# A second buffer for the transposed row maxima, and the loads for eight heads put in the queue over eight head steps

## The chip, the cores and the metric

One core of a Trainium2 chip runs the kernel. The metric is the device time of one execution in microseconds; the profile adds one execution with a record of every instruction.

## What is computed

Two independent branches on 2048 x 576 inputs, concatenated along the last axis.

```python
# A: 32 heads of width 18, sequence in N=4 segments of L=512
q,k,v = x@wq, x@wk, x@wv                     # split in heads and segments
for s in range(4):
    logits = qs @ ks.T * 18**-0.5 + mask     # mask: -1e9 where key > query ... within the segment
    a_dot  = softmax(logits) @ vs
    a_mem  = phi(qs) @ M / (phi(qs) @ z + 1e-6)
    o      = g*a_mem + (1-g)*a_dot           # g = sigmoid(beta), one per head
    M += phi(ks).T @ vs; z += sum(phi(ks))   # phi(t) = t+1 for t>0, exp(t) otherwise
out_a = o @ wo
# B: a filter in the frequency domain
out_b = irfft2(rfft2(x_B) * (w_r + 1j*w_i))
```

(The mask compares the indices inside a segment; the kernel keeps the entries it allows through a table of its own.)

## The kernel before

The program runs in stages. First the forward transform of branch B and the projections of branch A are interleaved; q, k, v go to scratch tensors in device memory (`qkD`, `reD`, `vD`, and `pqD` for phi(q)). Then the inverse transform of B is interleaved with a prologue of the attention. The last 360 us or so are the attention (`attention`, L938), and the change lies there.

The attention is a software pipeline of **head steps** `t` = 0 to 132, one head of one segment each. Four steps make a quad `k`, eight steps a **group** `n`, that is eight heads of one segment; there are 16 groups, and four of them make a segment `g`. In step `t` the program emits, in an order written out by hand:

- `s1` (L646) for the head eleven steps ahead: matmuls of Q and K, and on VectorE the maxima of each row of logits (L661, L667), into tiles `mx`, `mg`;
- `s2` (L694) for head `t`: matmuls L702, L706, L707, L711 of K and Q, which here have two more rows (108 and 109) that hold the row maxima and so subtract them, and on ScalarE the exponentials L703, L708, L712 into `P`; GpSimd zeroes the forbidden triangle (L716);
- `pv` (L731) for a quad some steps back, `pv_out` (L737) copies the result to `U`.

The row maxima get into rows 108 and 109 of Q by `mpath` (L675), once for each quad `k`, started two quads ahead. At the first step of the quad in progress VectorE and ScalarE finish the maxima and GpSimd splits them in two bf16 parts `mh` (L682, L683). At the second step TensorE transposes `mh` (L686) and ScalarE copies the result to `mts` (L689), of which there is one buffer. Two steps after that call's clock, which is the end of the third step of the quad, ScalarE issues the transfer from `mts` into Q (L692). `later(k, f)` puts a call off by k steps; `due(t)`, at the end of step `t`, makes the calls that have come due. In the prologue GpSimd issues that transfer (L691).

Loads for the steps to come stand in a list `q`. When a group begins (`t%8==0`) nine entries are appended (L960 to L963): four that load Q for the group two ahead (three pieces from `qkD`, L635, and the rest from `reD`, L637), four of the same kind that load K for the group three ahead, and the load of V for the group two ahead (`load_v`, L644). Each step takes one entry at its beginning (L982) and one at its end (L1005), so that the nine are in after four and a half steps. Q has three buffers, K four, V three. The Q just loaded is read first by `s1` at the sixth step of the same group (`t+11`); its buffer was last read by `s2` in the last step of the group before.

A second list, `qu`, is treated in the same way and holds the five stores of a finished group's `U` (L742 to `rD`, L747 to `uD`). They are appended at the end of the fourth step. All of these go to SyncE's (SP's) queue, and so do the loads of phi(q) (`pq`, L776), of unnormalized outputs (`ux`, L825), the chains of reciprocals (`recip`, L749: load L752, store L765, load L769), the stores of denominators (L790), some moves between tiles (L843, L844) and the stores of the output (`ya`, L877). SP works through its queue in program order and stands where a transfer has to wait for data or for a free buffer. Within the same part of the program only the `mts` transfer is in ScalarE's queue. In the program as built, every transfer of SP and ScalarE counts on one of eight semaphores that are dealt out in turn, in the order in which the framework's planner expects the issues; before an issue the queue waits until the transfer that had the same semaphore eight turns earlier has landed.

The tiles named `x` in the trace are those of Q, K and the mask that share one allocation (`x0`); `Qs<-mts` and `x<-mts` are the same line for different Q buffers.

Of the kernel before, what the change touches and what calls it, by code (L numbers as in the profile page):

```python
# [340 lines left out]
BF=mybir.dt.bfloat16  # L341
# [43 lines left out]
class ATT:  # L385
# [289 lines left out]
    def mpath(s,k):  # L675

        nc=s.nc; n,qd=divmod(k,2); Q=s.Qs[n%3]
        mx=s.mx.pop(k); mg=s.mg.pop(k)
        nc.vector.tensor_reduce(out=mg[:,:,2:3],in_=mx[:,:,:3],axis=mybir.AxisListType.X,op=OP.max)
        nc.scalar.copy(mg[:,:,0:1],mx[:,:,3:])  # L680
        mh=s.mh; mg=mg.rearrange("p h i -> p (h i)")
        nc.gpsimd.tensor_copy(mh[:,0],mg)  # L682
        nc.gpsimd.tensor_tensor(mh[:,1],mg,mh[:,0],op=OP.subtract)  # L683
        yield
        pt=s.psm.tile([128,1024],BF,name="mt",tag=s.mtag)[:,:128]
        nc.tensor.transpose(pt,mh.rearrange("p a m -> p (a m)"),s.idb)  # L686
        yield
        mt=s.sm.tile([32,128],BF,name="mts",bufs=1)
        nc.scalar.copy(mt,pt[:32])  # L689
        out=Q[108:110,4*qd:4*qd+4].rearrange("p h (i c) -> p (h i) c",c=128)  # L690
        if s.now<0: nc.gpsimd.dma_start(out,mt)  # L691
        else: s.later(2,lambda: nc.scalar.dma_start(out,mt))  # L692
        yield
# [244 lines left out]
    def attention(s,tp,ps):  # L938
        nc=s.nc; s.tp,s.ps,s.psm,s.mtag=tp,ps,s.ps1,"s1"
        s.homes()  # L940
        def steps(gen,i):
            for _ in range(i):
                try: next(gen)
                except StopIteration: return
        m=None
        q=[]
# [3 lines left out]
        def run_bg(rate):  # L950
            state["acc"]+=rate
            if state["acc"]>=1:
                state["acc"]-=1
                while bg:
                    try: next(bg[0]); break
                    except StopIteration: bg.pop(0)
        lane=[]
        for t in range(133):
            k,hh=divmod(t,4); n,qd=divmod(k,2); g=k//8
            if hh==0 and qd==0:  # L960
                if 0<n<14: q+=s.stack_dmas(n+2,0)
                if 0<n<13: q+=s.stack_dmas(n+3,1)
                if n+2<16: q.append(lambda n=n: s.load_v(n+2))  # L963
            st=t%32
            if 16<=t<21: s.pq_load(1,ORD[t-16])
            if t==34: bg.append(s.den(1,lane))
            if st==8 and g>0:
                def ln(g=g):
                    r=s.recip(s.rD[g-1],s.rrD[g-1],s.g1,False,"rr",2)
                    for i in range(8):  # L970
                        if 2<i<6: s.ux_load(g-1,ORD[i-3])
                        next(r); yield
                    yield from r
                    bg.append(s.mixed(g))
                    o=s.oproj(g-1)
                    if g<3: bg.append(itertools.islice(o,4)); bg.append(s.den(g+1,lane))
                    bg.append(o)
                lane.append(ln())
            if t==125: lane.append(s.recip(s.rD[3],s.rrD[3],s.g1,False,"rr"))
            a=s.s1(t+11) if t+11<128 else iter(())  # L980
            b=s.s2(t) if t<128 else iter(())
            if q: q.pop(0)()  # L982
            if qu: qu.pop(0)()
            steps(a,1)
            steps(b,1)
            run_bg(0)
            steps(a,1)
            steps(b,1)
            if 4<=t-1<132: s.pv((t-5)//4,(t-5)%4)
            run_bg(1.2)  # L990
            steps(a,1)
            if hh==1 and m is not None: steps(m,1)
            steps(b,1)
            if hh==1 and m is not None: steps(m,1)
            if hh==0 and k+2<32: m=s.mpath(k+2); next(m)
            if t>=7 and t%4==3:
                s.pv_out((t-7)//4)
                if t%8==3:
                    u=s.u_dmas((t-11)//8)
                    if t<124: s.later(1,lambda u=u: qu.extend(u))  # L1000
                    else: qu+=u
            for l in list(lane):
                try: next(l)
                except StopIteration: lane.remove(l)
            if q: q.pop(0)()  # L1005
            if qu: qu.pop(0)()
            s.due(t)
        assert not q
# [144 lines left out]
```

## Time and profile before

| | |
|---|---|
| median of 3 runs | 717.85 us (716.23 to 718.08) |
| profiled execution | 717.86 us, span 716.2 us, granted clock 0.997 |
| TensorE busy | 681.5 us, 95% of the span |
| VectorE busy | 551.0 us, 77% |
| ScalarE busy | 450.6 us, 63% |
| GpSimd busy | 210.0 us, 29% |
| SP's transfers (queue q1) | 106.89 MB, 59.1% of 16 DMA engines |

The profile tells for each instruction when it ran, how long its engine had been idle before it, and what released it ("1.15 <-ACT P L703": 1.15 us idle, ended by ScalarE's line 703). "PEld" is the load of weights into TensorE. "SPq" and "ACTq" are transfers issued by SP and ScalarE; the time in such a row is the issue, not the transfer. In the chain of work a row "DMA a<-b" has the time from issue to landing. A row of a stretch gives, after its length, the busy time and number of instructions of PE, PEld, DVE, ACT and POOL, the granted clock, the DMA share and GB/s.

### The profile page before, as it was taken

To read this page: it belongs to the slowest core of one execution; us is meant where nothing else is said; L and a number is where in the kernel's file an instruction comes from. 1 tells how busy PE (TensorE), PEld (TensorE's weight loads), DVE (VectorE), ACT (ScalarE), POOL (GpSimd) and SP (SyncE) were. 2 spreads that over 40 slices of the span, in tenths; PEclk is the share of its full clock that TensorE was granted. 3 is DMA by queue.
4 is the path that set the end of the run, shared out by engine and by line. 5 is a ranking of instruction groups with operands and counts; after the bars stand their busy time and mean duration, and the time that the engine had idled before them with its cause. 6 is when DMAs were issued, how large, how long until landed. Compare 5 with 4: busy or idle time off the path is not lost.

```text
span 716.2 us, 14406 instructions
## 1 busy us (share of the span) xinstructions
PE 681.5 (95%) x4991; PEld 501.8 (70%) x4991; DVE 551.0 (77%) x1262; ACT 450.6 (63%) x986; POOL 210.0 (29%) x403
## 2 busy tenths in 40 slices
PE   5999999999999999999999799899999999999997
PEld 4988769879779879999844354444666445663487
DVE  6999979899699789787687687887656876577533
ACT  3665796585586575443378587767666776567521
POOL 5532000100200111665145233434323652235300
PEclk9999999999999999999999999999999999999999
DMA  9995555675384778999249787997757968252152
GB/s 311 295 279 159 149 140 185 189 196 181 112 245 143 188 209 283 221 241 260 94 134 195 146 160 149 191 193 162 168 111 163 207 150 168 60 149 66 27 160 76
DMA packets 71146, 123.80 MB, mean 173 GB/s; under 512 B 12184, under 2 KB 39174, under 8 KB 67482
## 3 DMA queue, kind: packets, MB, share of 16 engines
q1 hardware_dynamic: 64422, 106.89, 59.1%
q0 software_dynamic: 5632, 15.76, 8.1%
q8 instruction: 39, 0.64, 0.4%
q10 hardware_dynamic: 1020, 0.25, 0.2%
q14 instruction: 33, 0.27, 0.2%
HBM read 82.10 MB, written 39.81 MB: 170 GB/s over the span
## 4 chain that ended last, share of the span: by engine, by line
PE 62%; DMA 12%; ACT 4%; DVE 3%; issue 3%; POOL 3%; SPq 1%; ACTq 0%; POOLq 0%; DVEq 0%
PE pj L461 12%; PE pjv L461 8%; PE s L653 8%; PE pv L731 7%; PE po L874 4%; PE i L306 3%; PE i L295 3%; PE s L702 3%; DMA x<-mts 2%; DMA yb<-yout 2%; PE s L706 2%; PE pn L804 2%; PE pm L529 2%; PE s L666 1%; PE s L711 1%
## 5 line engine op out<-in xcount | busy, mean ns | idle before, releaser
L661 DVE CUSTOM_DVE_ANT_0 junk<-s,x 128x512 bf16<-128x512 f32 x248 | 137.0, 552 | 64.2 <-PE s L653 59.6
L716 POOL TENSOR_SCALAR_AFFINE_SELECT P<-P 128x512 f32<-128x512 f32 (+2 forms) x132 | 78.4, 626 | 123.0 <-ACT P L703 113.5
L667 DVE TENSOR_REDUCE mx<-s 128x4 f32<-128x512 f32 x128 | 87.7, 685 | 5.5 <-PE s L666 3.6
L703 ACT ACTIVATE P<-s 128x512 f32<-128x512 f32 x128 | 77.7, 607 | 16.6 <-PE s L666 5.2
L731 PE MATMUL pv<-P,vs 128*32 128x512 f32 (+3 forms) x1024 | 83.8, 443 | 0.2
L708 ACT ACTIVATE P<-s 128x512 f32<-128x512 f32 x128 | 77.5, 605 | 2.6 <-PE s L707 2.4
L712 ACT ACTIVATE P<-s 128x256 f32<-128x256 f32 x128 | 49.9, 389 | 44.2 <-PE s L711 44.1
L653 PE MATMUL s<-Ks,Qs 108*128 108x384 bf16 (+3 forms) x256 | 69.0, 301 | 2.1 <-DVE mx L667 1.2
L731 PEld LDWEIGHTS pv<-P,vs 128*32 128x32 f32 x1024 | 27.1, 110 | 46.2 <-issue 34.5
L461 PE MATMUL pj<-x,wqkh 128*128 128x512 f32 x162 | 56.5, 409 | 0.0
L205 DVE TENSOR_TENSOR Z<-t,t 128x290 f32<-128x290 f32 (+1 forms) x96 | 48.4, 554 | 0.1
L653 PEld LDWEIGHTS <-Qs 108*128 108x128 bf16 x320 | 31.6, 99 | 23.5 <-issue 12.1
L519 POOL MEMSET vt<- 128x32 f32 x16 | 2.4, 167 | 149.5 <-PE pm L529 123.3
L205 DVE TENSOR_TENSOR t<-Z 128x580 f32<-128x580 f32 x64 | 46.1, 756 | 0.0
L142 PE MATMUL f<-ftab,eh 128*128 128x290 f32 (+1 forms) x160 | 32.3, 321 | 11.5 <-DMA ftab<-ftab 8.8
L666 PE MATMUL s<-tri,idb 128*128 128x128 bf16 x256 | 43.1, 220 | 0.0
L295 PE MATMUL i<-civ,Y 128*128 128x256 f32 (+1 forms) x288 | 39.3, 289 | 0.2 <-POOL Y L280 0.2
L295 PEld LDWEIGHTS i<-civ,Y 128*128 128x128 f32 (+1 forms) x288 | 36.6, 181 | 1.0 <-POOL Y L280 0.4
L306 PE MATMUL i<-itab,T 128*128 128x290 f32 (+1 forms) x224 | 36.7, 306 | 0.4 <-DVE yout L314 0.4
L142 PEld LDWEIGHTS f<-ftab,eh 128*128 128x128 f32 (+1 forms) x160 | 26.0, 206 | 13.8 <-ACT eh L126 7.4
L461 PE MATMUL pj<-x,wqkl 128*128 128x512 f32 x90 | 35.6, 395 | 0.0
L461 PE MATMUL pj<-xh,wqkl 128*128 128x512 f32 x90 | 35.5, 395 | 0.0
(210 smaller groups left out, 1830.8 us busy)
## 6 DMA issues: line engine op xcount, KB each, us to landing
qkD<-sp SPq DMA_DIRECT2D x32, 384.0 KB
xin<-xb SPq DMA_DIRECT2D x16, 384.0 KB
cfw<-cfw POOLq DMA_DIRECT2D x16, 384.0 KB, 4.4
civ<-civ POOLq DMA_DIRECT2D x16, 384.0 KB, 9.2
vs<-vD SPq DMA_DIRECT2D x16, 330.0 KB
vD<-vt SPq DMA_DIRECT2D x16, 311.0 KB
W<-w SPq DMA_DIRECT2D x16, 290.0 KB
yb<-yout SPq DMA_DIRECT2D x16, 290.0 KB
```

The source lines that it names most:

```text
L142: nc.tensor.matmul(p[:,r,:FP],x,t,start=n==0,stop=n==6)
L205: v.tensor_tensor(o,a,b,op=op)
L295: nc.tensor.matmul(p[:m,k],Y[i][:,q,c*128:c*128+m],cc[:,hl,o:o+256],start=n==0,stop=n==5)
L306: nc.tensor.matmul(p,x,t,start=n==0,stop=n==6)
L461: s.nc.tensor.matmul(out,a,b,start=i==0,stop=i==len(L)-1)
L653: nc.tensor.matmul(out,Q[:108,h,128*i:128*i+128],K[:108,h,:128*(i+1)],start=True,stop=True)
L661: nc.vector.tensor_tensor_reduce(out=junk[:,:w],in0=src,in1=s.mask[:,512-w:],scale=1.0,scalar=-3.0e38, op0=OP.add,op1=OP.max,accum_out=s.m ...
L667: nc.vector.tensor_reduce(out=s.mx[k][:,hh],in_=pa.rearrange("p (b c) -> p b c",c=128),axis=mybir.AxisListType.X,op=OP.max)
L703: nc.scalar.activation(P[0][:,hh],p0,AF.Exp,scale=SC)
L708: nc.scalar.activation(P[1][:,hh],p1,AF.Exp,scale=SC)
L716: nc.gpsimd.affine_select(out=x[:,r],in_=x[:,r],pattern=[[0,r.stop-r.start],[1,128]],compare_op=OP.is_ge,fill=0.0,base=0,channel_multiplie ...
L731: nc.tensor.matmul(s.pvt[32*hh:32*hh+32,128*j:],vt[:,j,19*h:19*h+32],mv[0][:,hh,mv[1]],start=j==0,stop=j>1,skip_group_check=True)
```

## The change

`mts` gets two buffers instead of one, and the entry of `q` at the end of a step is taken only when `t%8==0`. The nine entries of a group thus go in two in the first step and one in each of the other seven.

```diff
@@ mpath
-        mt=s.sm.tile([32,128],BF,name="mts",bufs=1)
+        mt=s.sm.tile([32,128],BF,name="mts",bufs=2)
         nc.scalar.copy(mt,pt[:32])
         out=Q[108:110,4*qd:4*qd+4].rearrange("p h (i c) -> p (h i) c",c=128)
         if s.now<0: nc.gpsimd.dma_start(out,mt)
@@ attention, end of a step
-            if q: q.pop(0)()
+            if q and t%8==0: q.pop(0)()
             if qu: qu.pop(0)()
             s.due(t)
```

## The prediction

> **What bounds the kernel now.** I read the page first, then the chain in order of time, the waits, and the timeline around the places where the chain leaves the matmuls.
>
> ```profile
> PE 681.5 (95%) x4991; PEld 501.8 (70%) x4991; DVE 551.0 (77%) x1262; ACT 450.6 (63%) x986; POOL 210.0 (29%) x403
> PE 62%; DMA 12%; ACT 4%; DVE 3%; issue 3%; POOL 3%; SPq 1%; ACTq 0%; POOLq 0%; DVEq 0%
> ```
>
> TensorE is busy 95% of the span, so only about 35 us of it can be won by shortening waits, and nothing in this change shortens a matmul. What the change can touch are waits for transfers, and the chain says where these end last:
>
> ```profile
> 390.35 7.16 DMA Qs<-reD
> ...
> 397.59 8.78 DMA x<-mts
> ...
> 406.39 0.26 ACT mts L689
> ```
>
> Read downwards: the last Q load of a group lands after 7.16 us; only then can ScalarE issue the transfer out of mts (L692); that one needs 8.78 us; only then can ScalarE write the next row maxima into the single mts buffer (L689). The same place in the timeline, and in the stretches:
>
> ```profile
> 395.12 0.39 ACT L712 ACTIVATE P<-s 128x256 f32<-128x256 f32 x1
> 397.59 0.62 ACTq L692 DMA_DIRECT2D x<-mts  x1
> 398.90 0.38 PE L702 MATMUL s<-Qs,Ks 110*128 110x512 bf16 x1 [1.15 <-ACT P L703]
> 399.99 0.32 PE L653 MATMUL s<-x,Qs 108*128 108x384 bf16 x1
> 406.39 0.26 ACT L689 COPY mts<-mt 32x128 bf16<-32x128 bf16 x1 [2.85 <-DMA x<-mts]
> 406.69 0.27 PE L653 MATMUL s<-x,Qs 108*128 108x256 bf16 x1 [2.58 <-ACT mts L689]
> ```
> ```profile
> 389.00:398.00 9.00, 7.99 (x73) 4.01 (x72) 7.38 (x27) 5.52 (x15) 3.47 (x6) 1.00 0.98 183
> 398.00:407.00 9.00, 5.35 (x44) 2.71 (x44) 4.63 (x14) 5.17 (x13) 2.82 (x6) 1.00 0.90 186
> 452.00:461.00 9.00, 7.20 (x64) 3.81 (x66) 8.06 (x24) 6.55 (x18) 5.03 (x12) 1.00 0.94 188
> 461.00:470.00 9.00, 8.52 (x86) 4.29 (x78) 6.87 (x22) 7.14 (x17) 3.31 (x7) 1.00 0.93 190
> 470.00:479.00 9.00, 8.68 (x74) 4.33 (x70) 8.06 (x25) 6.39 (x15) 3.64 (x7) 1.00 0.93 192
> 479.00:490.00 11.00, 9.96 (x84) 4.96 (x87) 8.26 (x24) 7.71 (x19) 4.29 (x8) 1.00 0.89 191
> ```
>
> From 398 to 407 TensorE, VectorE and ScalarE are all half idle (5.35, 4.63 and 5.17 of 9 us): nobody has work in hand that would make up for it later, so this time is lost to the end. The DMA engines are 0.90 to 0.98 busy there, hence the slow landings.
>
> **The change part by part.**
>
> *Two mts buffers.* No instruction is added; a copy into mts need no longer wait for the transfer four head steps earlier. The larger of such waits, in total, times and longest:
>
> ```profile
> ACT mts L689 <- DMA x<-mts: 3.8, 2, 2.8
> PE s L653 <- ACT mts L689: 3.5, 3, 2.6
> ```
>
> ScalarE loses 3.8 us in two places, TensorE 3.5 us in three behind it. The largest is the 2.58 us above; the next is this one:
>
> ```profile
> 458.91 0.26 ACT L689 COPY mts<-mt 32x128 bf16<-32x128 bf16 x1 [0.93 <-DMA x<-mts]
> 459.22 0.27 PE L653 MATMUL s<-Ks,Qs 108*128 108x256 bf16 x1 [0.66 <-ACT mts L689]
> ```
>
> The transfer itself must then land only before the L702 matmul that reads it, six head steps after its issue. The slowest took 9.6 us (tile view of mts):
>
> ```profile
> DMA to landing us min/median/max: 3.7/6.7/9.6
> ```
> ```profile
> 416.42 0.62 ACTq L692 DMA_DIRECT2D Qs<-mts  x1
> 424.21 0.62 ACTq L692 DMA_DIRECT2D Qs<-mts  x1
> ```
>
> In a quiet group two such issues, four steps apart, lie 7.8 us apart. Six steps are 11.7 us, so nothing new waits. Gain 2.6 + 0.7 + 0.2 = 3.5 us.
>
> A stall of this length costs more than itself. Behind it the granted clock falls to 0.50 for some microseconds (the column before the DMA share):
>
> ```profile
> 407.00:416.00 9.00, 9.00 (x73) 4.26 (x72) 6.13 (x19) 6.00 (x16) 2.87 (x6) 0.81 0.53 117
> 408.00:409.00 1.00, 1.00 (x10) 0.40 (x12) 0.75 (x3) 0.93 (x2) 0.49 (x1) 0.50 0.04 10
> ```
>
> At 0.81 over nine microseconds, 9 x 0.19 = 1.7 us are missing. With the 2.58 us gone I take the 1.7 us as gained too (bounds 0 and 1.7); no other stretch of the attention that I asked for has a granted clock under 1.00. [...]
>
> *The spread.* Three Q pieces, Q rest (reD), three K pieces, K rest and V go in over eight steps: Q0 Q1 | Q2 | Qr | K0 | K1 | K2 | Kr | V, where before they went Q0 Q1 | Q2 Qr | K0 K1 | K2 Kr | V. Count, bytes and queue are the same; only SP's order against its other transfers changes, and through that the wait at L692. Each transfer of the SP and ACT queues counts on one of eight semaphores dealt in turn, so its issue waits until the one eight turns earlier has landed. SP's part in turn order around the stall, before:
>
> ```profile
> 388.66 0.78 SPq L635 DMA_DIRECT2D Qs<-qkD  x2
> 389.54 0.36 SPq L776 DMA_DIRECT2D pq<-pqD  x1
> 389.94 0.37 SPq L635 DMA_DIRECT2D Qs<-qkD  x1
> 390.35 0.39 SPq L637 DMA_DIRECT2D Qs<-reD  x1
> 390.78 0.36 SPq L776 DMA_DIRECT2D pq<-pqD  x1
> 391.19 0.84 SPq L635 DMA_DIRECT2D Ks<-qkD  x2
> ```
>
> SP runs ahead of ScalarE, so the mts turn of step 18 stands behind pq (step 20). Eight back from there are pq, Kr, K2, pq, K1, K0, pq, Qr: the Qr load, as the chain says. After the change Qr, K0 and K1 each slip a step, K2 and Kr go behind rD<-U, where SP stops for the copy of U, and the mts turn stands behind K1: eight back are K1, pq, K0, pq, Qr, pq, Q2, pq(17), the transfer issued at 389.54. By the same 7.16 us it lands at 396.7; that is 0.9 us sooner than 397.51, and the load ahead of it is smaller by Q2 and Qr, so between 0.9 and the whole 2.08 us (395.51 to 397.59) of ScalarE's wait goes. On TensorE this is up to 1.15 us; I take 1.0.
>
> What is late next is Q itself. Its last piece landed at 397.51 and is first read at 399.99: 2.5 us of cover, of which the removed 1.0 us of stall takes some. In the new order one more pq goes before Qr. Its size and that of a V load:
>
> ```profile
> vs<-vD SPq DMA_DIRECT2D x16, 330.0 KB
> ...
> pq<-pqD SPq DMA_DIRECT2D x12, 252.0 KB
> ```
>
> At the 183 GB/s of that stretch pq is 1.4 us. Cover 1.5 against 1.4: from 0 to 1 us lost; I take 0.3. In the other groups Qr slips only where something waits between it and Q2 (a store of ob, a pq load), one step at most, and those steps hold more work on TensorE, which lengthens the cover as well.
>
> K and V have 7 and 14 steps until they are read, 13.6 us and more at 7.8 us per four, so their delay costs nothing by itself. On SP's queue K2, Kr and V are moved past the rD and uD stores and, in the groups that have them, past ux loads and the stores of the reciprocals. The stores gain from that. V comes to stand directly before the next group's Q0: where SP has been standing at a store of reciprocals, Q lands up to 330 KB or 1.8 us later, and the cover of 2.5 us holds it.
>
> The second mts transfer of a group (step 6 of 8) gets a nearer neighbour: eight back are now V, uD, Kr, uD, uD, K2, uD, rD, the rD store of step 4, where it was mostly a load or a store one to three turns older. These waits cannot be seen before; nearest are the one that did wait, on a uD store, and the shortest distance from rD to it:
>
> ```profile
> 455.90 1.22 SPq L747 DMA_DIRECT2D uD<-U  x2
> 461.33 0.62 ACTq L692 DMA_DIRECT2D x<-mts  x1
> ```
> ```profile
> 419.89 0.55 SPq L742 DMA_DIRECT2D rD<-U  x1
> ```
>
> The uD store took 5.4 us in a busy stretch (DMA share 0.94); rD has 4.3 us, to the issue at 424.21, in a quiet group. At the 3.7 us that the quickest mts transfer took it is free; at 5.4 us it costs 1.1 us of ScalarE each time. Quiet groups have drained queues, so I am nearer to 3.7 and take 0.7 us in all (bounds 0 and 9, below).
>
> Sum: gains 3.5 + 1.7 + 1.0 = 6.2; costs 0.3 + 0.7 = 1.0; net -5.2 us. The profiled execution took 717.86 us (span 716.2 and 1.7 around it), the median of the runs is 717.85. Forecast 717.86 - 5.2 = 712.7 us. With the terms at their worse bounds (3.5 gained, no clock, no spread, 1 each for Q and the second transfers) it is 716.4 us; with no costs and half of the way to the first rival below, 709.7 us.
>
> **The rivals.** About 0.3%, 2.15 us, is what a measurement of this kernel can tell from no change, so 715.7 and 720.0 are the borders.
>
> *More is reclaimed.* If all idle time of TensorE from 389 to 490 belongs to these two waits, it is 1.01 + 3.65 + 1.80 + 0.48 + 0.32 + 1.04 = 8.3 us, and 1.7 of clock: 717.86 - 10.0 = 707.9 us. Against it: in 452 to 461 VectorE is busy 8.06 of 9, so part of that idle time is VectorE's.
>
> *The spread gives back the largest stall.* If Q lands 2.6 us late at step 21, TensorE idles as before and the clock falls again; what is left is 1.0 + 0.7 + 0.2 - 0.7, or little more: about -1.5 us, 716.4 us. It decides when Qr lands after about 399. For it: a DMA share of 0.98 in this stretch; against it: K0 and K1 no longer follow at once.
>
> *Slower: the second transfer of each group waits.* If rD takes the 5.4 us of the busy stretch in all twelve groups that are loaded, ScalarE stands 1.1 us each; TensorE lost 0.66 of 0.93 us in the row above, so 0.71 x 1.1 x 12 = 9.4 us. With -5.2 that is +4.2: 722.1 us. It decides where rD lands later than 4.3 us after its issue. For it: the uD row; against it: the loads queued ahead of rD in its group shrink from nine to six.
>
> *The change does not do what it says* holds in part: SP runs ahead until something blocks it, so in quiet groups the first six loads still go in one burst. I count it in the forecast: only the order matters.
>
> **How the numbers follow.** Forecast 0.50, more reclaimed 0.10, given back 0.18, slower 0.22. Faster than 715.7: 0.50 + 0.10 + 0.04 of the third = 0.64. Slower than 720.0: 0.20 of the last. Same: 0.16. Range: half of the second case lies below 708.0 (0.05), somewhat over half of the last above 721.5 (0.13), so 708.0 to 721.5; the forecast alone is 709.7 to 716.4.
>
> **What would show it.** Right: no copy at L689 waits for a transfer; the mts issue of step 18 stands within 1 us of the activation ahead of it; no clock of 0.50 after it; PE idle in the stretch of steps 18 to 21 falls from 3.65 us to about 1. Wrong: idle time at L653 that ends with a Qs load at step 21, or ScalarE standing before the mts issues of step 6 of the groups, released by rD. I would be wrong altogether if the steps after 22 grew by what was won, with VectorE or ScalarE idle for transfers.

## The result and the profile after

The kernel after takes 711.11 us (median of 6 runs, 709.38 to 714.06), the kernel before 717.56 us beside it (6 runs, 716.23 to 721.57): a ratio on record of 0.9882, 95% interval 0.9846 to 0.9918, which also holds the quotient of the two medians, 0.9910. The forecast was 712.7 us. The profiled execution of after took 710.93 us, 6.93 less than that of before.

The page of after, busy time and the chain by engine:

```profile
PE 679.2 (96%) x4991; PEld 501.4 (71%) x4991; DVE 551.2 (78%) x1262; ACT 451.3 (64%) x986; POOL 209.8 (30%) x403
PE 36%; DMA 3%; DVE 3%; ACT 2%; POOL 2%; issue 2%; ACTq 0%; SPq 0%; DVEq 0%; POOLq 0%
```

TensorE does the same 4991 matmuls in 2.3 us less busy time (behind the stall of before, at half clock, 16 matmuls of L731 took 2.36 us, elsewhere 1.28). The shares of the two chains can't be compared as they stand, because the chain of after can be followed back only to 369 us, that of before to 87. From 369 us on the longer transfers in the chain add up to 66.6 us before and to 19.7 us after.

The timeline of after from step 18 to step 22, the place of the stall (start, duration, and in brackets the idle time before with what ended it):

```profile
394.49 0.39 ACT L712 ACTIVATE P<-s 128x256 f32<-128x256 f32 x1
395.15 0.62 ACTq L692 DMA_DIRECT2D x<-mts  x1
398.11 0.32 PE L653 MATMUL s<-x,Qs 108*128 108x384 bf16 x1
401.18 0.24 ACT L689 COPY mts<-mt 32x128 bf16<-32x128 bf16 x1
402.43 0.39 ACT L712 ACTIVATE P<-s 128x256 f32<-128x256 f32 x1
404.31 0.62 ACTq L692 DMA_DIRECT2D x<-mts  x1
404.98 0.60 ACT L703 ACTIVATE P<-s 128x512 f32<-128x512 f32 x1 [2.17 <-PE s L711]
```

The transfer out of mts of step 18 is issued 0.27 us after the activation ahead of it (before: 2.08). The copy of step 21 comes at 401.18 with no idle time before it; before it came at 406.39 after 2.85 us of waiting. Q is first read at 398.11 without a wait. New is the second issue: the activation of step 22 ends at 402.82, the issue stands until 404.31, 1.49 us, and ScalarE does not go on until 404.98. The chain of after names what that issue waited for:

```profile
397.71 6.53 DMA rD<-U
```

The wait for transfers out of mts that is left, and their landing (tile view; before 3.7/6.7/9.6):

```profile
PEld L702 <- DMA x<-mts: 0.3, 1, 0.3
DMA to landing us min/median/max: 2.4/5.7/9.1
```

No copy into mts waits for a transfer any more, and only once does a matmul wait for rows 108 and 109, by 0.3 us (at 650 us, near the end). The same stretches as before (length, busy time of PE, PEld, DVE, ACT, POOL, granted clock, DMA share, GB/s); ahead of them the one of before that the prediction does not show:

```profile
443.00:452.00 9.00, 9.00 (x91) 4.55 (x84) 8.00 (x24) 6.24 (x16) 2.84 (x7) 1.00 0.88 161
```

```profile
389.00:398.00 9.00, 8.18 (x76) 4.03 (x73) 7.32 (x26) 7.08 (x18) 4.17 (x8) 1.00 1.04 203
398.00:407.00 9.00, 8.34 (x78) 4.46 (x78) 7.37 (x23) 5.92 (x16) 2.65 (x7) 1.00 0.72 164
407.00:416.00 9.00, 8.68 (x83) 4.40 (x82) 7.29 (x25) 7.38 (x20) 3.86 (x8) 1.00 0.99 195
443.00:452.00 9.00, 7.86 (x72) 3.83 (x71) 8.36 (x24) 7.38 (x19) 4.54 (x11) 1.00 0.98 190
452.00:461.00 9.00, 9.00 (x85) 4.90 (x84) 7.79 (x24) 7.00 (x18) 3.36 (x8) 1.00 0.80 203
461.00:470.00 9.00, 8.19 (x75) 4.04 (x73) 7.70 (x23) 6.45 (x17) 4.06 (x7) 1.00 0.96 196
470.00:479.00 9.00, 8.27 (x59) 4.02 (x62) 7.12 (x22) 6.73 (x15) 3.89 (x7) 1.00 0.81 207
479.00:490.00 11.00, 10.95 (x95) 5.38 (x88) 8.92 (x26) 8.40 (x20) 4.82 (x10) 1.00 0.70 158
```

In 389 to 416 TensorE idles 0.82 + 0.66 + 0.32 = 1.80 us where before it idled 1.01 + 3.65 + 0 = 4.66, and the 1.7 us of half clock are gone: 4.6 us won. In 443 to 490 it idles 1.14 + 0 + 0.81 + 0.73 + 0.05 = 2.73, before 0 + 1.80 + 0.48 + 0.32 + 1.04 = 3.64: 0.9 us. Together 5.5 of the 6.9 us. About 1 us of the rest lies ahead of step 13, where the two executions already stand 0.9 us apart counted from the first copy into mts (317.60 before, 317.91 after); most other kernels' profiles stand between 1.0 us less and 0.4 us more than before at that point, so I give it to no step.

A second measure, free of where the slices are cut, is the time between two copies into mts (L689), from their start times. It serves for all kernels below, one profile each (us). The medians stand beside it; each ratio, as on record, is to the kernel before of its own series. The quotients of the medians differ from these ratios by up to 0.003 and lie inside the intervals.

| kernel | steps 13-17 | 17-21 | 21-25 | 41-45 | 45-57 | 57-117 | median us | ratio to before (interval) |
|---|---|---|---|---|---|---|---|---|
| before | 8.8 | 12.5 | 9.0 | 10.4 | 28.8 | 165.6 | 717.56 | |
| after | 8.8 | 7.9 | 9.0 | 9.4 | 28.5 | 165.7 | 711.11 | 0.9882 (0.9846-0.9918) |
| after, again | 8.8 | 8.7 | 8.3 | 9.4 | 28.0 | 165.6 | 711.68 | 0.9898 (0.987-0.9926) |
| two buffers alone | 11.8 | 7.9 | 8.9 | 9.4 | 30.1 | 165.8 | 715.17 | 0.9952 (0.9932-0.9971) |
| spread alone | 8.8 | 10.5 | 7.5 | 9.4 | 28.1 | 165.6 | 713.74 | 0.992 (0.9897-0.9942) |
| own turns, two buffers, old order | 9.6 | 7.8 | 7.8 | 9.4 | 28.1 | 165.7 | 710.43 | 0.9882 (0.986-0.9903) |
| own turns, two buffers, spread | 8.8 | 9.0 | 7.8 | 9.4 | 28.0 | 165.6 | 710.73 | 0.9889 (0.986-0.9919) |
| own turns, one buffer, old order | 8.5 | 10.5 | 9.1 | 10.0 | 27.9 | 165.6 | 716.42 | 0.9967 (0.9942-0.9993) |

From step 57 to step 117 nothing differs by over 0.2 us in these kernels: most of the matter is the loaded steps 13 to 57, and most of that the eight steps 17 to 25. A quad without a wait takes 7.8 us there. Three differences lie outside the columns. Steps 1 to 13 take 25.8 us in own turns with one buffer and 24.4 to 24.9 in the others. Steps 25 to 41 take 34.8 us in own turns with the spread, where TensorE stands 1.62 us for a Q load, and 34.0 in own turns with one buffer, against 33.1 to 33.4 in the others. And after step 117 own turns with the spread is 1.0 us or more longer than the others; the granted clock of its whole profile is 0.996, against 1.000 and 0.999 in the two of after.

### The profile page after: what moved, and what is told of

Same layout as the page of the kernel before. It is cut to its first block, busy times and chain, and to the rows that moved or that the text cites. A ratio compares the mean times of both kernels' runs of the same rounds, so it can differ in the third digit from the quotient of the medians.

```text
span 709.2 us, 14404 instructions
## 1 busy us (share of the span) xinstructions
PE 679.2 (96%) x4991; PEld 501.4 (71%) x4991; DVE 551.2 (78%) x1262; ACT 451.3 (64%) x986; POOL 209.8 (30%) x403
## 5 line engine op out<-in xcount | busy, mean ns | idle before, releaser
L731 PE MATMUL pv<-P,vs 128*32 128x512 f32 (+3 forms) x1024 | 82.5, 439 | 0.1
L653 PE MATMUL s<-Ks,Qs 108*128 108x384 bf16 (+3 forms) x256 | 69.1, 301 | 1.5 <-DVE mx L667 1.2
L731 PEld LDWEIGHTS pv<-P,vs 128*32 128x32 f32 x1024 | 26.9, 109 | 45.3 <-issue 34.5
L653 PEld LDWEIGHTS <-Qs 108*128 108x128 bf16 x320 | 31.5, 98 | 24.4 <-issue 13.0
L142 PE MATMUL f<-ftab,eh 128*128 128x290 f32 (+1 forms) x160 | 32.6, 323 | 11.8 <-DMA ftab<-ftab 9.2
```

The lines of the kernel that those rows point to most:

```text
L142: nc.tensor.matmul(p[:,r,:FP],x,t,start=n==0,stop=n==6)
L653: nc.tensor.matmul(out,Q[:108,h,128*i:128*i+128],K[:108,h,:128*(i+1)],start=True,stop=True)
L731: nc.tensor.matmul(s.pvt[32*hh:32*hh+32,128*j:],vt[:,j,19*h:19*h+32],mv[0][:,hh,mv[1]],start=j==0,stop=j>1,skip_group_check=True)
```

## The experiments

*Two buffers alone.*

```diff
-        mt=s.sm.tile([32,128],BF,name="mts",bufs=1)
+        mt=s.sm.tile([32,128],BF,name="mts",bufs=2)
```

> The kernel before with two mts buffers and nothing else. My theory (buffer and turn are two separate waits, and the half clock belongs to the stall at the copy): no copy at L689 waits for a transfer; ScalarE still stands about 2 us before the mts issue of step 18, for the Qr load; the granted clock stays at 1.00 behind it; 3.5 + 1.7 = about 5 us less than before, 712 to 713.5 us, ratio 0.993. Rival (the gain comes from the thinner loads): under 2 us less than before, ratio above 0.997. Rival (the half clock has another cause): the clock still falls to 0.5 near 408 us and the gain is about 3.5 us.

Measured: 715.17 us, 3.5 us less than before (718.68 in this series); less than the working theory expected. The timeline at steps 14 and 22, and the stretch around:

```profile
386.75 0.38 ACT L712 ACTIVATE P<-s 128x256 f32<-128x256 f32 x1
388.74 0.62 ACTq L692 DMA_DIRECT2D Qs<-mts  x1
389.41 0.60 ACT L703 ACTIVATE P<-s 128x512 f32<-128x512 f32 x1 [2.27 <-DMA vs<-vD]
390.06 0.38 PE L702 MATMUL s<-Qs,Ks 110*128 110x512 bf16 x1 [1.85 <-ACT P L703]
...
405.28 0.39 ACT L712 ACTIVATE P<-s 128x256 f32<-128x256 f32 x1
407.12 0.62 ACTq L692 DMA_DIRECT2D x<-mts  x1
```
```profile
389.00:398.00 9.00, 7.62 (x51) 3.48 (x50) 4.70 (x17) 6.83 (x17) 4.16 (x7) 0.81 1.05 194
398.00:407.00 9.00, 9.00 (x91) 4.54 (x89) 8.10 (x25) 6.06 (x15) 2.81 (x6) 1.00 0.92 172
```

No copy waits for a transfer, and the quad of steps 17 to 21 falls from 12.5 to 7.9 us as with the whole change. The half clock behind the copy of step 21 is gone too (1.00 from 398 to 416). But the issues of the transfer still stand for their turns, 1.6 us at step 14 (a V load) and 1.45 us at step 22. At steps 46 and 54 they stand 1.82 and 2.23 us (0.93 and 1.74 in before), which fits the 30.1 us of steps 45 to 57. The wait at step 14 stops TensorE for 1.85 us and has a half clock of its own behind it (0.81 from 389 to 398), so that the quad ahead takes 3.0 us more than before. The turn is that of the kernel before: counted along the queues, the same issue has the same V load eight turns back, and there it did not have to wait for it. How often it does is not settled by one profile of each.

*The spread alone.*

```diff
-            if q: q.pop(0)()
+            if q and t%8==0: q.pop(0)()
```

> The loads over eight steps, one mts buffer. My theory: the mts issue of step 18 no longer waits for Qr, but the copy of step 21 still waits for that transfer to land, about 2 us, and the clock falls behind it; 1 to 2 us less than before, ratio 0.997 to 0.999. Rival (the thinner loads bring the gain, by a shorter landing): the copy hardly waits, and the time is that of the whole change, ratio 0.988 to 0.990.

Measured: 713.74 us, 4.9 us less than before; more than expected. The timeline at steps 18 and 21, and the stretch behind:

```profile
397.20 0.62 ACTq L692 DMA_DIRECT2D x<-mts  x1
397.87 0.60 ACT L703 ACTIVATE P<-s 128x512 f32<-128x512 f32 x1 [1.19 <-DMA pq<-pqD]
405.50 0.25 ACT L689 COPY mts<-mt 32x128 bf16<-32x128 bf16 x1 [1.80 <-DMA x<-mts]
405.80 0.27 PE L653 MATMUL s<-x,Qs 108*128 108x256 bf16 x1 [1.52 <-ACT mts L689]
407.00:416.00 9.00, 9.00 (x91) 4.49 (x89) 7.57 (x23) 7.20 (x17) 3.51 (x8) 1.00 0.91 187
```

The turn now ends with a pq load, as predicted, not with Qr. The copy still waits for the transfer, but 1.80 us instead of 2.85, and TensorE idles 1.52 instead of 2.58. Of the 2.1 us by which the quad of steps 17 to 21 is shorter, 1.6 come from the sooner issue (2.16 us after the copy of step 17, before 3.72) and 0.5 from the time between the issue and the next copy (8.30, before 8.80). No half clock follows: the quad of steps 21 to 25 falls from 9.0 to 7.5 us. So this share of the clock cannot be put down to the buffers alone. And at steps 41 to 45 each edit alone wins the 1.0 us that both together win once. Whether the times of whole kernels add up is not shown: the medians give 3.5 and 4.9 us for the edits one by one and 6.45 together, with intervals of 1.4 to 2.6 us to either side.

*Turns of its own.* The transfer out of mts is put in GpSimd's queue, which takes it out of the eight semaphores that it shares with SP's loads (in the trace of before the last Q load at the stall, landing at 397.51, and the transfer out of mts behind it, landing at 406.37, count on the same one of these): first with two buffers and the old order, then added to the whole change.

```diff
-        else: s.later(2,lambda: nc.scalar.dma_start(out,mt))
+        else: s.later(2,lambda: nc.gpsimd.dma_start(out,mt))
```

> Two mts buffers, the loads over four and a half steps as before, and the mts transfer of the attention in GpSimd's queue, whose transfers count on semaphores of their own, so that no mts issue has to wait for a load and none of ScalarE's time goes into it. My theory (what the spread brings is the semaphore turn alone): as fast as the whole change or faster, 709 to 711.5 us, ratio 0.988 to 0.991. Rival (the spread relieves the DMA engines, and that is what counts): it stays 1 to 2 us slower than the same with the spread (the next run), near two buffers alone, ratio 0.993.

> The whole change with the mts transfer of the attention in GpSimd's queue. In the changed kernel ScalarE still stands 1.5 us before the mts issue of step 22, for rD<-U. My theory: this wait goes too, 1 to 1.5 us less than the whole change, 709 to 710 us, ratio 0.987, and no difference beyond 1 us to the same with the old order of loads. Rival (a queue on GpSimd costs as much as it brings, because its transfers are slower or stand behind the triangle work): ratio 0.990 or more.

Measured: 710.43 and 710.73 us, against 718.68. In the tile views of both no issue at L692 waits for a transfer; the waits before it, 21 in each, end with the copy into mts. With the old order of the loads, two buffers and turns of its own the stretches of the stall are full:

```profile
398.00:407.00 9.00, 9.00 (x91) 4.49 (x91) 8.16 (x26) 6.72 (x17) 4.44 (x9) 1.00 0.97 183
407.00:416.00 9.00, 9.00 (x85) 4.88 (x85) 7.75 (x24) 6.92 (x18) 4.67 (x10) 1.00 1.01 220
```

The DMA share is as high as ever (0.97 and 1.01), the nine loads go in as quickly as before, and still two quads of 7.8 us follow each other. So the stall can go without any thinning of the traffic: what the spread does there is to move the transfers on which the issue at L692 has to wait. Where that wait is gone, the spread brings nothing more that these runs could tell (0.9889 against 0.9882, the intervals overlap nearly whole; a difference under some 2.5 us would not show). One thing is not separated: this edit also takes the issue, 0.62 us each, out of ScalarE's queue, and the transfers land sooner in the median (4.8 us, against 6.3 with the two buffers alone).

*Turns of its own with one buffer*: the same line, and `bufs=1` with the old order, to see whether the single buffer only hands the turn's delay on.

> The kernel before with one line changed: the transfer out of mts goes through GpSimd's queue (L692), with the one mts buffer and the old order of the loads. Theory A, the shared turn is the root and the single buffer only hands its delay on: the issue of step 18 comes at about 395.5 us instead of 397.59, lands by 404 even at 8.8 us, and the copy of step 21 waits for it by less than 0.7 us; -5 to -7 us, ratio about 0.990. Theory B, the single buffer is the root (a transfer of 8.8 us is too long for four head steps whenever it is issued): the copy of step 21 still waits over 1.5 us and the gain is at most 2 us, ratio about 0.998.

Measured: 716.42 us against 718.30, a gain of 1.9 us (by the interval of the ratio 0.5 to 4.2): the second theory. The issue (by GpSimd) and the copy behind it:

```profile
396.02 0.61 POOL L692 DMA_DIRECT2D x<-mts  x1 [1.25 <-ACT mts L689]
406.03 0.25 ACT L689 COPY mts<-mt 32x128 bf16<-32x128 bf16 x1 [2.65 <-DMA x<-mts]
406.34 0.27 PE L653 MATMUL s<-x,Qs 108*128 108x256 bf16 x1 [2.38 <-ACT mts L689]
```

The issue comes 0.5 us after the copy of step 17 (395.49 in this profile); in before it came 3.7 us after it (393.87 to 397.59). The transfer lands at 406.0 all the same, after 10 us. In all, copies wait 6.0 us for transfers in six places here, in before 4.2 us in three. A quad without a wait lasts 7.8 us, so a single buffer cannot do with a transfer of that length, whenever it is issued. Both causes are real: the slow transfer needs the second buffer, and the turns need the new order (or turns of their own). With only one of the two mended, 1.9 to 4.9 us are won, with both 5.8 to 8.3 (the medians of all such kernels here).

*The clock.* In the whole change the copy of step 21 is repeated, 14 times or 7 times, so that ScalarE is held with no transfer involved; beside it the kernel after again, unchanged.

```diff
-        nc.scalar.copy(mt,pt[:32])
+        for _ in range(14 if k==7 else 1): nc.scalar.copy(mt,pt[:32])
```

> The kernel after, with the copy from mt to mts done 14 times in place of once at one quad (the copy of step 21, L689), so that ScalarE is held there by 13 x 0.24 = 3.1 us, with no transfer involved. Theory A, a gap of this length halves the granted clock behind it: TensorE idles 2.5 to 3 us, a stretch of 0.50 of about 3.4 us follows, and the time grows by the gap and 1.7 us: +4 to +4.7 us against the kernel after. Theory B, the clock drop of the kernel before had another cause: no 0.50 behind the gap, +2.5 to +3 us.

> As the longer hold, but 7 copies: ScalarE is held by 6 x 0.24 = 1.4 us at step 21. [...] If any gap over 1 us costs clock, a 0.50 follows and it grows by about 3 us. If the loss of the gap is made up later, it grows by less than 0.5 us.

> The kernel after, unchanged, on the same chip as the two holds so that they are compared with it: 711 us, ratio 0.988 to the kernel before. A second profile shows which of its waits are the same from one execution to the next: the turn wait of step 22 for the rD store (1.5 us of ScalarE) should come back if it belongs to the order of the queue, and not if it was that execution's traffic.

Measured: long 715.41 us, short 712.57, after 711.68. The long hold, its gap and the microseconds behind it:

```profile
400.90 3.96 ACT L689 COPY mts<-mt 32x128 bf16<-32x128 bf16 x14
405.41 0.38 PE L702 MATMUL s<-Qs,Ks 110*128 110x512 bf16 x1 [2.60 <-ACT P L703]
406.00:407.00 1.00, 1.00 (x11) 0.32 (x12) 0.70 (x2) 1.00 (x3) 0.34 (x1) 0.80 0.88 269
407.00:408.00 1.00, 1.00 (x12) 0.21 (x4) 0.00 (x0) 0.06 (x1) 1.00 (x3) 0.50 0.11 29
408.00:409.00 1.00, 1.00 (x9) 0.55 (x6) 0.41 (x2) 0.20 (x1) 0.46 (x1) 0.50 0.00 0
409.00:410.00 1.00, 1.00 (x6) 0.50 (x5) 0.58 (x3) 0.73 (x3) 0.63 (x1) 0.50 0.29 57
410.00:411.00 1.00, 1.00 (x10) 0.72 (x9) 0.84 (x3) 1.00 (x2) 0.00 (x0) 1.00 1.01 262
```

A gap of 2.60 us that ScalarE alone makes is followed by 0.50, for 0.4 + 3.0 = 3.4 us (the first slice at 0.80 is 0.4 us at half). The two stretches of 9 us say what that costs:

```profile
398.00:407.00 9.00, 6.05 (x53) 2.90 (x55) 5.42 (x18) 7.86 (x26) 1.54 (x5) 0.98 0.73 173
407.00:416.00 9.00, 9.00 (x77) 4.54 (x73) 6.21 (x19) 6.10 (x16) 2.62 (x7) 0.83 0.72 135
```

The clock lacks 9 x 0.02 + 9 x 0.17 = 1.7 us, TensorE idles 2.95 us instead of 0.67 and 0 instead of 0.31 (the same stretches of after, again): 2.3 - 0.3 + 1.7 = 3.7 us. Steps 17 to 25 take 20.6 us, in the repeat of after 17.0. The medians differ by 3.73 us; the two profiled executions by only 1.86, as that of the long hold is 1.2 us ahead at step 17 and gains another 0.5 behind step 25. So in this profile the half clock is paid in full, and it comes behind a gap made by ScalarE alone, with no transfer in the way. The hold of half the length is 0.9 us above the repeat in the median, within the spread of the runs, and its stretches keep a clock of 1.00. But the longest gap of TensorE behind it is 0.59 us, so it says nothing of longer ones.

A gap of TensorE in each of five profiles, and the granted clock behind it:

| kernel | gap, us | ends at, us | clock behind it |
|---|---|---|---|
| long hold | 2.60 | 405.41 | 0.50 for 3.4 us |
| before | 2.58 | 406.69 | 0.50 for 3.41 us, from 407.86 |
| own turns, one buffer, old order | 2.38 | 406.34 | 0.83 from 406 to 407, then 0.50 to 410 |
| two buffers alone | 1.85 | 390.06 | 0.81 from 389 to 398, or 3.4 us at half |
| spread alone | 1.52 | 405.80 | 1.00 |

The half clock begins 0.3 us (own turns with one buffer) to 2.0 us (two buffers alone) after the end of the gap. The 1.62 us of own turns with the spread, at 417.37, cost no more than themselves: steps 25 to 41 are 1.4 to 1.7 us longer there than where they take 33.1 to 33.4. That the length of the gap decides alone is not shown. In own turns with the spread and in own turns with Q sooner (below) the granted clock of the whole profile is 0.996, although it is 1.00 from 389 to 416 and from 443 to 490; what stood ahead of the missing part is not shown. Nor does one profile of before tell whether every execution of it loses the 1.7 us.

*Q sooner.* Two more entries early, so that Q is in after two steps; with turns of its own, and with the shared ones.

```diff
-            if q and t%8==0: q.pop(0)()
+            if q and t%8<2: q.pop(0)()
```

> The kernel after with two more lines changed: the transfer out of mts goes through GpSimd's queue, and the entry at the end of a step is taken at the first two steps of a group (t%8<2), so that Q is in the queue after two steps and K and V follow one a step. What still stopped TensorE with own turns were Q loads (0.8 to 1.6 us at one or two places). Theory A, with the turns out of the way only the lateness of Q is left: 1 us less than the same kernel with the even spread, 709 to 710 us, ratio 0.987. Theory B, what is left belongs to VectorE, GpSimd and traffic: 710.5 to 711.5 us, ratio 0.989.

> The kernel after with the entry at the end of a step taken at the first two steps of a group (t%8<2); the transfer out of mts stays in ScalarE's queue and shares the turns. Q is in the queue after two steps, one step sooner, and Qr stands nearer to the mts issue of the same group's third step. Theory A, a turn wait for a Q load comes back there: 712 to 715 us, slower than the kernel after. Theory B, the number of loads in the queue is what counts: as the kernel after, 711 us, ratio 0.990.

Measured: 710.55 us (ratio 0.989, 0.9865 to 0.9915) and 712.62 us (0.9914, 0.9893 to 0.9935). With shared turns the issue of step 18 stands 0.9 us, and the row names a Q load:

```profile
396.64 0.39 ACT L712 ACTIVATE P<-s 128x256 f32<-128x256 f32 x1
397.93 0.62 ACTq L692 DMA_DIRECT2D x<-mts  x1
398.60 0.60 ACT L703 ACTIVATE P<-s 128x512 f32<-128x512 f32 x1 [1.56 <-DMA Qs<-qkD]
```

That fits the turns: the same two buffers and as few loads, but a Q load eight turns back. It does not show that this order is worse there, for in the repeat of after the same issue stands 1.25 us (below). As a whole kernel it is 0.9 us above that repeat, with overlapping intervals. With turns of its own, the profile of Q sooner has little left of the waits for Q, one of 0.5 us (a matmul) and one of 0.7 us (a load of weights) from 360 to 660: its quads from 17 to 25 take 7.8 us each and steps 25 to 41 33.1 us. The medians with Q sooner and without, 710.55 and 710.73 us, show nothing of the 1 us expected. No kernel here is shown to be faster than after.

## Why the prediction was right, and where its sizes were off

*The place and the sum.* For the stall at steps 18 to 22 the prediction had 2.6 + 1.7 + 1.0 - 0.3 - 0.7 = 4.3 us, TensorE's stretches give 4.6. For the later place it had 0.7 + 0.2, and 0.9 came (by the copies of steps 41 to 57 it is 1.3, in the repeat 1.8). The median of after lies 1.6 us below the forecast, within its own runs (709.38 to 714.06); the 0.9 us ahead of step 13 in the profile belong to no term. Two small slips in the working move nothing: from 397.51 to 396.7 is 0.8 us, not 0.9, and halfway to the first rival is 709.8 us, not 709.7.

*The buffers.* The 3.5 us of waits at L653 went, and nothing new waits at L702 but 0.3 us once. As predicted. What the prediction did not see is that with the buffers alone ScalarE's turn waits stay and move: step 14 cost 3.0 us in that profile, and the whole kernel won 3.5 us instead of the 3.5 + 1.7 that were booked with the buffers.

*The spread: the term that was mis-sized.* It stood at 1.0 us, and alone it is worth 4.9. The row for the step was right (the turn ends with pq, the copy's wait falls by 1.05 us, TensorE's by 1.06), but the quad of steps 17 to 21 is 2.1 us shorter, since the 1.15 us of TensorE behind the late issue go as well as the 1.06 at the copy. Two more things hang on the spread that had been booked elsewhere: the clock of the quad behind (9.0 to 7.5 us), given to the buffers although 1 us less of gap was enough in that profile, and the 1.0 us at steps 41 to 45, booked with the buffers at 0.7, which again either edit wins (10.4 to 9.4 us). And 0.6 us at 45 to 57 (28.75 to 28.14) had not been booked. There the prediction had overlooked a wait: it named one second transfer of a group that stood before the change, that of step 46 (0.93 us), but that of step 54 stood 1.74 us (activation to 478.69, issue at 480.43), with 0.65 us of TensorE behind it. After the change neither stands over 0.3 us. In the sum of both edits the size came out, since the shares at the stall and at steps 41 to 45 were each booked once. That it came out so close is partly luck: the wait overlooked (0.6 us won) and a cost booked too low (0.7 us, below up to 1.2) about cancel.

*The clock.* The prediction took the 1.7 us as gained, with 0 as the other bound. For this profile that was right: with the gap gone, TensorE idles 0.66 us from 398 to 407 (0.67 in the repeat), and the clock is 1.00 from 389 to 416 in both profiles of after. Both bounds were possible all the same: the long hold lost 1.7 us of clock behind a gap of 2.60 us, but the spread alone lost none behind 1.52 us, and these rows do not show what decides between them.

*Q late* was booked at 0.3 us. In the first profile of after Q is read at 398.11 without a wait. In the repeat, the first load of weights from it waits:

```profile
399.73 0.10 PEld L653 LDWEIGHTS <-Qs 108*128 108x128 bf16 x1 [0.61 <-DMA Ks<-qkD]
```

The row names a K load; K is not due for steps, so I take it for a Q piece whose semaphore a K load shares, which no run here tells apart. Between 0 and 0.6 us in after, the 0.3 stands. With turns of its own and the spread, the first read of a Q eight steps further on stands 1.62 us for a Q load in the one profile, over the 1 us that was the bound:

```profile
417.37 0.32 PE L653 MATMUL s<-Ks,Qs 108*128 108x384 bf16 x1 [1.62 <-DMA Qs<-qkD]
```

That profile took 714.52 us and the median of the kernel is 710.73, so it is no rule.

*The second transfer of each group.* The slower rival has its mechanism in the trace, at one group: 1.49 us of ScalarE at step 22, ended by the rD store that took 6.53 us, over the 4.3 us from which it decides, and over the 5.4 us that was its bound. The repeat has it too, 0.81 us from the activation to the issue:

```profile
404.10 0.39 ACT L712 ACTIVATE P<-s 128x256 f32<-128x256 f32 x1
405.30 0.62 ACTq L692 DMA_DIRECT2D x<-mts  x1
405.96 0.60 ACT L703 ACTIVATE P<-s 128x512 f32<-128x512 f32 x1 [1.47 <-DMA rD<-U]
```

So it belongs to the order. It is part of why the quad of steps 21 to 25 takes 8.3 to 9.0 us, up to 1.2 above 7.8, and eats what the clock gave back there. The cost was booked at 0.7 us in all groups; it is up to 1.2 in one, and next to nothing in the other eleven: no second transfer there stands over 0.3 us in either profile of after, and the steps from 57 to 117 take as long as before (165.6 and 165.7 us). The rival failed in its factor of twelve.

*The signs.* No copy waits: so. PE idle from 398 to 407 down to about 1: 0.66. No 0.50: so. The issue of step 18 within 1 us of the activation ahead: 0.27 us in the first profile, but in the repeat the activation ends at 395.75 and the issue comes at 397.00:

```profile
395.36 0.39 ACT L712 ACTIVATE P<-s 128x256 f32<-128x256 f32 x1
397.00 0.62 ACTq L692 DMA_DIRECT2D x<-mts  x1
```

That is 1.25 us, and the quad of steps 17 to 21 takes 8.7 us there. This turn wait is shortened, not removed, and how much of it is left depends on the execution. In the two holds, which keep this order of the loads, it is 0.48 and 0.66 us, and their rows name the pq load that the prediction had counted out.

*More is reclaimed* held in the main where it said that all idle time around the stall belongs to these waits (3.65 fell to 0.66, and to 0 with turns of its own), not in 443 to 490, where 2.73 of 3.64 us stayed. *The spread gives back the largest stall* did not come about.

## What to carry to other kernels

Here a small transfer shared eight semaphores, dealt in turn, with a busy queue, and its issue waited for whatever stood eight turns back (2.08 us for the last Q load in before, 1.49 us for a store to rD in after). In a like kernel ask which transfer that is before and after an edit, and remember that reordering loads moves that neighbour as well as the loads. A buffer that is filled once per period needs a second one as soon as the slowest transfer out of it is longer than the period (here 10 us against 7.8). A wait that several edits can shorten, and the half clock behind it, is won by whichever comes first; book it once, and look for the other places where the same wait stands. A gap of TensorE can cost more than itself (here 1.7 us of clock behind 2.58 us): read the granted clock of the stretch behind it, and do not take what one profile shows there for every execution.

## What the runs showed of the hardware

In four profiles TensorE's granted clock stood at 0.50 for 3.4 us, beginning 0.3 to 2.0 us after gaps of 1.85 us (two buffers alone), 2.38 us (own turns with one buffer), 2.58 us (before) and 2.60 us (long hold); behind the 1.52 us of the spread alone it stayed at 1.00. In before, where TensorE was busy throughout those 3.41 us, that is 1.7 us lost, as in the long hold. And the transfer out of mts, 32 rows of 128 bf16 values, took up to 10.5 us to land from either queue while loads were queued on SP: at most 8.6 to 9.8 us in the profiles where ScalarE issued it and 9.7 to 10.5 us where GpSimd did. The medians differ the other way, 5.4 to 6.7 us and 3.7 to 4.8 us; whether the queue makes that, or the moment of the issue, no run here tells.
